# Weight operands made in two lanes, q's softmax with one exp, and another distance ahead of TensorE's matmuls in the planner

## The chip, the cores and the metric

The kernel runs on one core of a Trainium2 chip. The metric is the time of one execution on the device in microseconds. A core has five engines that each work off their own instructions in order: TensorE (PE, matmuls), VectorE (DVE), ScalarE (ACT), GpSimd (POOL) and SyncE (SP, which here issues nearly all DMAs). They wait for each other by semaphores.

## The reference

```python
def _attn_ref(q, k, v):                      # 8 batches, 8 heads, 576 rows, 64 columns
    q_s = q - np.max(q, axis=-1, keepdims=True)
    q_s = np.exp(q_s)
    q_s = q_s / (np.sum(q_s, axis=-1, keepdims=True) + 1e-09)
    k_s = k - np.max(k, axis=2, keepdims=True)
    k_s = np.exp(k_s)
    k_s = k_s / (np.sum(k_s, axis=2, keepdims=True) + 1e-09)
    kv = np.einsum('bhsd,bhse->bhde', k_s, v)
    return np.einsum('bhsd,bhde->bhse', q_s, kv)
def _moe_ref(x, w_in, w_out):                # 4608 tokens, 512 to 2048 to 512
    r = np.maximum(x @ w_in, 0.0)
    return (r * r) @ w_out
def _moe2_ref(x, w_gate, w_val, w_out):      # 512 to 1536 to 512
    g = x @ w_gate
    return (g * (1.0 / (1.0 + np.exp(-g))) * (x @ w_val)) @ w_out
```

Attention's output, heads side by side, is the x of the first MLP, and its output the x of the second.

## The kernel before

**Tiles.** The 4608 tokens are nine blocks of 512. A float32 matrix is split into a high part (a cast to fp32r, on ACT) and a low part (what the cast left, on DVE); a product is then three matmuls: high by high, high by low, low by high (`mm3`, all of them on line 107). The weights arrive as 8-byte numbers, and `bits` makes float32 words of them (one ACT and three DVE operations on 128x512).

**Stages.** (1) A first block, whose order is written out by hand (`FIRST_BLOCK`): block 0's attention, the conversion of the first MLP's weights, block 0 through the first MLP. (2) The direct stage: blocks 1 to 4 through the first MLP, with attention of the later blocks in between. (3) The pairs: blocks 5 to 8, two and two, by a scheme that replaces eight products of quarter matrices by seven (`PRODUCTS`). It needs sums and differences of quarters of the weights as operands. (4) The second MLP with the same seven products, in five groups of blocks (`gated` for gate and val, then `out_stage`).

**Weight operands.** `prepare` makes the operands of the seven products from 34 sets: 16 of the first MLP (their words are in memory already), 12 of gate and val, 6 of the second `w_out`. For a set it loads two halves, makes words (`bits`), forms sums (`quarter_sums`, line 325 on DVE), splits (`parts`, called by `staged`: ACT line 287, DVE line 289) into a staging tile `wst`, and stores that to memory (`hd`, `ad` for the first MLP, `gvd`, `od` for the second). The sets go one after the other. Operands for the matmuls are fetched in 512 KB pieces (tiles `wu`, five slots, line 829) on SP's queue.

**The planner.** Stages 2 and 3 get their order from `Plan`: each unit of work is a chain of steps (engine, assumed duration, what it needs, what it frees), with a rank. `Plan.run` takes the step that could start earliest, and among steps of that engine within 0.3 the lowest rank. The matmuls of the main line have rank 3, attention's 2 and something, the weight operands 5. `after` is the time that the plan leaves between an engine's end and its successor on another engine: 0.9 ahead of any PE step. What the plan puts out is then the fixed order on all five engines. In `gated` of the first group (g == 0) `next(work, None)` issues what is left of `prepare`, six steps behind each product, its stores on ACT's queue.

**Attention in the plan.** `kv_unit`: maxima of k on DVE, a transpose on PE (line 598), a reduction, a transpose back (604), a subtraction on DVE, an exp on ACT (612), 24 matmuls (557). `q_unit`: maxima on DVE (642), eight exps of 128x64 on ACT with the maximum as bias and the sum as second output (647), a reciprocal, a product on POOL (654), four transposes (678), the matmuls with kv.

Of the kernel before, what the change touches and what calls it, by code (L numbers as in the profile page):

```python
# [22 lines left out]
def tile_linear_attention_two_mlps(  # L23
# [30 lines left out]
    def f32(ap):  # L54
        return ap.bitcast(F32)
# [140 lines left out]
    class Plan:  # L196
# [26 lines left out]
        def start(self, u):  # L223
            engine, _, needs, take = u[2][:4]
            s = max(self.free[engine], u[3] + self.after(u[4], engine))
            for x in needs:
                if x not in self.done:
                    return None
                t, e = self.done[x]
                s = max(s, t + self.after(e, engine))  # L230
            for pool, key in take:
                bufs, keys = self.pools[pool]
                n = len(keys) - bufs
                if n >= 0:
                    x = pool, keys[n]
                    if x not in self.done:
                        return None
                    t, e = self.done[x]
                    s = max(s, t + self.after(e, engine))
# [40 lines left out]
    made = set()  # L280
    prep = {"stages": [(stp, "wst")] + [(raws, "raw0"), (raws, "raw1")], "raws": [], "n": 0, "r": 0}
# [9 lines left out]
    def staged(source, dests, by_rows=False, free=(), key=None):  # L291

        k_ = len(dests)
        pool, tag = prep["stages"][prep["n"] % len(prep["stages"])]
        prep["n"] += 1
        keep = (tag, prep["n"])
        prep["last"][tag] = [prep["n"]]
        t = []

        def make():  # L300
            t.append(pool.tile([P, 2, 2, U], F32R, name="wst", tag=tag))
# [19 lines left out]
    def quarter_sums(m, n, by_rows):  # L321
# [5 lines left out]
        yield step("DVE", 0.8)  # L327
# [6 lines left out]
        yield step("DVE", 0.8)  # L334
# [7 lines left out]
    def half_words(n):  # L342
        return cv.tile([P, T], F32, name="wsum", tag=f"wb{n}")

    def prepare():

        sets = [
            (kind + "1", f)
            for half in range(2) for kind in ("in", "out") for f in range(half * NM // 2, (half + 1) * NM // 2)
        ]  # L350
        sets += [x for f in range(NG) for x in (("gate", f), ("val", f))] + [("out", f) for f in range(NG)]
        loaded = {}

        def first_load(s, x):
            kind, f = sets[s]
            yield step("SP", 0.6, (), [(f"wb{x}", s)], (), [("ld", s, x)], 4.0)
            loaded[s, x] = half_words(x)
            nc.sync.dma_start(loaded[s, x], w1d[kind[:-1]][f][:, x])

        def raw(s, x):  # L360
            kind, f = sets[s]
            w, by_rows = {"gate": (w_gate, False), "val": (w_val, False), "out": (w_out2, True)}[kind]
            tag = prep["raws"][prep["r"] % len(prep["raws"])]
            prep["r"] += 1
# [4 lines left out]
            loaded[s, x] = t, keep  # L369

        def bits(s, x):
            yield step("ACT", 0.67, [("ld", s, x)], [(f"wb{x}", s)])
            t, keep = loaded.pop((s, x))
# [3 lines left out]
            w = cv.tile([P, T], I32, name="wbits", tag=f"wb{x}")  # L377
            nc.scalar.activation(f32(w), f32(high), AF.Copy, scale=2.0**-112)
            yield step("DVE", 0.5)
# [11 lines left out]
            loaded[s, x] = f32(w)  # L391

        for x in (0, 1):
            yield from first_load(0, x)
        for s, (kind, f) in enumerate(sets):
            first = kind[-1] == "1"
            more = s + 1 < len(sets)
            if not first and not prep["raws"]:
                prep["stages"].remove((raws, "raw0"))
                prep["raws"].append("raw0")  # L400
                plan.pools["raw0"] = [1, []]
                yield step("DVE", 0.05, [("st", *sets[s - 1], x) for x in range(2)])
                yield from aside(raw(s, 0))
            if len(prep["raws"]) == 1 and prep["plan"] and ("x1", NB - 1, NP - 1) in plan.done:
                prep["stages"] += [(qtp, "qT0"), (qtp, "qT1")]
                plan.pools.update(qT0=[1, []], qT1=[1, []])
                yield step("DVE", 0.02, [("raw1", n) for n in prep["last"]["raw1"]])
                prep["stages"].remove((raws, "raw1"))
                prep["raws"].append("raw1")
                plan.pools["raw1"] = [1, []]  # L410
            keys = [("wb0", s)], [("wb1", s)]
            if first:
                yield step("DVE", 0.02, [("ld", s, 0), ("ld", s, 1)])
                m, n = loaded.pop((s, 0)), loaded.pop((s, 1))
                by_rows = kind == "out1"
                yield from quarter_sums(m, n, by_rows)

                def to(name):
                    return first_to(kind[:-1], f, name)

                todo = ((m, ("6", "5")), (n, ("4", "7"))) if by_rows else ((m, ("7", "3")), (n, ("5", "6")))
                for x, (source, names) in enumerate(todo):
                    yield from staged(source, [to(name) for name in names], False, keys[x], ("st", kind, f, x))
                    if more and sets[s + 1][0][-1] == "1":
                        yield from aside(first_load(s + 1, x))
            else:
                by_rows = kind == "out"
                yield from bits(s, 0)
                yield from aside(raw(s, 1))
                m = loaded.pop((s, 0))  # L430
# [6 lines left out]
                def out_of(source, names, free=(), key=None):  # L437
                    return staged(source, [to(name) for name in names], by_rows, free, key)
# [5 lines left out]
                yield from bits(s, 1)  # L444
# [1218 lines left out]
```

## Time and profile before

| | |
|---|---|
| time, median of 3 runs | 1724.65 us (1724.08 to 1727.84) |
| the profiled execution | 1727.46 us, span 1725.7 us |
| PE, DVE, ACT, POOL busy | 1651.0, 1116.6, 961.1, 223.2 us |
| first block ends, pairs begin, second MLP begins | about 125, 585.4 and 909.1 us |
| granted TensorE clock, mean | 0.99 |

PE is busy for 96% of the span, and its matmul records are pipelined, so busy is not the same as at its peak. What is lost is to be looked for stretch by stretch: where PE waits, and where its clock is not 1.00.

### The profile page before, as it was taken

The numbers are of one execution on the slowest core, as the hardware profiler recorded it, in microseconds if no ns is written. First come the engines' busy times: TensorE is split into PE (matmuls) and PEld (weight loads), VectorE is DVE, ScalarE is ACT, GpSimd is POOL, SyncE is SP. The second block draws the span as 40 slices with busy tenths as digits, with TensorE's granted clock in tenths as the row PEclk, the third lists the DMA queues.
The fourth block names the chain that finished last, engine by engine and source line by source line (L and its number), as shares of the span: only waits on it lengthen the run. The fifth ranks groups of instructions, "written<-read, shape, count | busy, mean of one in ns | idle before, by whom it ended". The sixth has DMA issues, their size and how long they took to land.

```text
span 1725.7 us, 24332 instructions
## 1 busy us (share of the span) xinstructions
PE 1651.0 (96%) x8210; PEld 1348.8 (78%) x8210; DVE 1116.6 (65%) x1923; ACT 961.1 (56%) x1972; POOL 223.2 (13%) x206
## 2 busy tenths in 40 slices
PE   7998899999989999999998789999999999999998
PEld 5777677777867878778786578888888888888898
DVE  8875454655557566887688867744774476456656
ACT  7775566665656885767565445433543354334434
POOL 4760000000000100000001111011101110111020
PEclk9999999999999999999999899999999999999999
DMA  9956686774556779898988788876786668666897
GB/s 302 285 171 187 183 240 200 210 241 136 164 166 212 227 249 339 329 324 283 364 298 297 268 280 280 246 214 192 218 251 209 196 217 255 202 193 207 248 390 264
DMA packets 275020, 420.02 MB, mean 243 GB/s; under 512 B 126288, under 2 KB 167248, under 8 KB 274896
## 3 DMA queue, kind: packets, MB, share of 16 engines
q1 hardware_dynamic: 268736, 408.10, 74.2%
q10 hardware_dynamic: 6160, 10.36, 1.6%
q8 instruction: 66, 1.08, 0.2%
q14 instruction: 58, 0.48, 0.1%
HBM read 317.19 MB, written 101.19 MB: 242 GB/s over the span
## 4 chain that ended last, share of the span: by engine, by line
PE 75%; ACT 6%; DMA 5%; DVE 5%; issue 2%; POOL 1%; SPq 0%; ACTq 0%; DVEq 0%; POOLq 0%
PE ps L107 56%; PE ph L107 9%; PE acc L107 6%; PE pa L557 1%; ACT qs L647 1%; PE pa L107 1%; DMA wu<-gvd 1%; DMA gvd<-wst 1%; ACT r L724 1%; DMA od<-wst 1%; ACT r L722 1%; ACT g L287 1%; DMA vt<-in_v_dram 1%; PE pa L678 1%; ACT wst L287 0%
## 5 line engine op out<-in xcount | busy, mean ns | idle before, releaser
L107 PE MATMUL ps<-w,wu 128*128 128x512 f32 (+1 forms) x3192 | 687.9, 377 | 26.2 <-DMA wu<-gvd 15.5
L107 PEld LDWEIGHTS ps<-w,wu 128*128 128x128 f32 x3192 | 570.1, 191 | 140.4 <-ACT ps L1235 7.0
L107 PE MATMUL ps<-uo,wu 128*128 128x512 f32 (+1 forms) x1932 | 418.3, 378 | 0.3 <-DVE uo L1097 0.3
L107 PEld LDWEIGHTS ps<-uo,wu 128*128 128x128 f32 x1932 | 345.6, 188 | 71.4 <-DVE uo L1097 2.1
L107 PE MATMUL ph<-xT,w 128*128 128x512 f32 x960 | 250.6, 404 | 0.6 <-DVE xT L1487 0.3
L107 PE MATMUL acc<-g,w 128*128 128x512 f32 x960 | 245.4, 400 | 0.8 <-DVE g L1509 0.8
L107 PEld LDWEIGHTS ph<-xT,w 128*128 128x128 f32 x960 | 178.4, 191 | 41.5 <-DVE xT L1487 0.9
L107 PEld LDWEIGHTS acc<-g,w 128*128 128x128 f32 x960 | 177.9, 190 | 40.5 <-DVE g L1509 1.2
L101 ACT CAST uo<-u 128x512 fp32r<-128x512 f32 (+1 forms) x210 | 119.9, 579 | 111.6 <-PE ps L107 42.4
L1288 POOL TENSOR_TENSOR u<-u 128x512 f32<-128x512 f32 (+1 forms) x30 | 35.5, 1185 | 958.4 <-DVE u L1284 958.4
L1283 DVE TENSOR_TENSOR u<-u,ps 128x512 f32<-128x512 f32 (+1 forms) x60 | 37.9, 632 | 184.5 <-ACT u L1282 184.4
L102 DVE TENSOR_TENSOR uo<-u,uo 128x512 fp32r<-128x512 f32 (+1 forms) x210 | 133.0, 651 | 31.8 <-ACT uo L101 31.6
L1235 ACT COPY ps<-ps 128x512 f32<-128x512 f32 x126 | 72.1, 574 | 128.7 <-PE ps L107 124.1
L289 DVE TENSOR_TENSOR g<-r,g 128x512 fp32r<-128x512 f32 x64 | 44.3, 692 | 117.1 <-ACT g L287 117.1
L654 POOL TENSOR_TENSOR qs<-qs,qr 128x512 f32<-128x512 f32 x28 | 32.0, 1142 | 462.6 <-DMA gvd<-wst 80.4
L1097 DVE TENSOR_TENSOR uo<-u,uo 128x512 fp32r<-128x512 f32 x112 | 73.3, 686 | 23.6 <-ACT uo L1095 23.4
L722 ACT ACTIVATE r<-ph 128x512 f32<-128x512 f32 x64 | 38.3, 598 | 88.2 <-PE ph L107 87.7
L1095 ACT CAST uo<-u 128x512 fp32r<-128x512 f32 x112 | 66.4, 620 | 23.8 <-PE ps L107 22.7
L647 ACT ACTIVATE qs<-qs,qm 128x64 f32<-128x64 f32 x224 | 75.1, 337 | 7.7 <-DVE qm L642 5.2
L287 ACT CAST wst<-wbits 128x512 fp32r<-128x512 f32 (+1 forms) x72 | 51.0, 715 | 36.8 <-DVE wbits L388 22.4
L289 DVE TENSOR_TENSOR wst<-wbits,wst 128x512 fp32r<-128x512 f32 (+1 forms) x72 | 56.4, 789 | 22.2 <-ACT wst L287 20.6
L1282 ACT ACTIVATE u<-ps 128x512 f32<-128x512 f32 (+1 forms) x60 | 33.3, 555 | 49.7 <-PE ps L107 48.1
(186 smaller groups left out, 1780.7 us busy)
## 6 DMA issues: line engine op xcount, KB each, us to landing
wu<-gvd SPq DMA_DIRECT2D x210, 512.0 KB, 4.5
wu<-od SPq DMA_DIRECT2D x105, 512.0 KB, 4.1
wu<-hd SPq DMA_DIRECT2D x56, 512.0 KB, 6.0
wu<-ad SPq DMA_DIRECT2D x56, 512.0 KB, 4.8
gvd<-wst SPq DMA_DIRECT2D x84, 256.0 KB, 4.0
od<-wst ACTq DMA_DIRECT2D x39, 256.0 KB, 4.8
w<-in_moe_w_in_dram SPq DMA_DIRECT2D x16, 512.0 KB, 6.4
w<-in_moe_w_out_dram SPq DMA_DIRECT2D x16, 512.0 KB, 6.8
```

The lines of the kernel that those rows point to most:

```text
L101: nc.scalar.copy(hi, src)
L102: (eng or nc.vector).tensor_tensor(lo, src, f32(hi), op=ALU.subtract)
L107: nc.tensor.matmul(ps, lhsT=w[s], rhs=x[t], start=start and n == 0, stop=stop and n == 2, skip_group_check=more,)
L287: nc.scalar.copy(hi, src)
L289: nc.vector.tensor_tensor(lo, src, f32(hi), op=ALU.subtract)
L647: nc.scalar.activation(t[:, x, h], t[:, x, h], AF.Exp, bias=m[:, x, h:h + 1], accum_out=r[:, x, h:h + 1])
L722: nc.scalar.activation(r, ph, AF.Relu)
L1095: nc.scalar.copy(t[:, 0], src())
L1097: nc.vector.tensor_tensor(t[:, 1], src(), f32(t[:, 0]), op=ALU.subtract)
L1235: nc.scalar.copy(x, y)
L1283: nc.vector.tensor_tensor(u, u, gate, op=ALU.mult)
L1288: nc.gpsimd.tensor_tensor(s1, a21, a22, op=ALU.add)
```

## The change

1. The weight operands are made in two lanes that draw from the same list (`Lane`, `lane_one`, `lane_two`) instead of one after the other. The second lane has its words in `raw0` first; once the last q is through it uses q's tiles and a tile of kv (`qs`, `qT0`, `qT1`, `kvs`). Each lane alternates between two staging tiles.
2. All 34 sets stand in the plan (the added `plan.run` over all stores): none is left for `gated`.
3. In `q_unit` POOL adds the negated maxima, one exp of 128x512 runs on ACT, and DVE sums.
4. `after` gives 0.4 ahead of PE steps of rank 3, and 1.7 ahead of the others, instead of 0.9. Some assumed durations of DVE, PE and POOL steps change by 0.02 to 0.2.

```diff
-        def after(self, engine, other):
+        def after(self, engine, other, rank):
             if engine is None or engine == other:
                 return 0.0
-            return {"PE": 0.9, "SP": 1.0}.get(other, 0.2)
+            return {"PE": 0.4 if rank == 3 else 1.7, "SP": 1.0}.get(other, 0.2)
...
+    to_do = iter(sets)
+    class Lane:
+        def __init__(self, halves, raw, stages):
+            self.halves, self.raw, self.stages = halves, raw, stages
+            self.n = 0
+        def stage(self):
+            self.n += 1
+            return self.stages[self.n % len(self.stages)]
...
+    def lane_one():
+        yield from lane_a.first_sets()
+        yield step("DVE", 0.02, [("st", "out1", NM - 2, 1), ("st", "out1", NM - 1, 1)])
+        yield from lane_a.second_sets()
+    def lane_two():
+        yield from lane_b.first_sets()
+        yield step("DVE", 0.02, [("x1", NB - 1, NP - 1)])
+        lane_a.stages = [lane_a.stages[0], slot(qtp, "qT0")]
+        kv_slot = kvs[0].rearrange("p a b c -> p (a b c)").rearrange("p (k h n) -> p k h n", k=2, h=2)
...
+        lane = Lane(
+            [("qs", q_spare), ("qs", q_spare)], "raw1",
+            [slot(qtp, "qT1"), ("kvs", lambda: kv_slot)],
+        )
+        yield from lane.second_sets()
...
         m = sp.tile([P, TJ, 2], F32, name="qm", tag="qm")
         nc.vector.tensor_reduce(m, t, axis=AX.X, op=ALU.max, negate=True)
+        yield step("POOL", 1.2)
+        nc.gpsimd.tensor_tensor(t, t, m.unsqueeze(3).to_broadcast([P, TJ, 2, D]), op=ALU.add)
+        yield step("ACT", 0.63)
+        nc.scalar.activation(t, t, AF.Exp)
+        yield step("DVE", 0.68)
         r = sp.tile([P, TJ, 2], F32, name="qr", tag="qr")
-        for x in range(TJ):
-            yield step("ACT", 0.6)
-            for h in range(2):
-                nc.scalar.activation(
-                    t[:, x, h], t[:, x, h], AF.Exp, bias=m[:, x, h:h + 1], accum_out=r[:, x, h:h + 1]
-                )
+        nc.vector.tensor_reduce(r, t, axis=AX.X, op=ALU.add)
...
-        plan.unit(work, 5, 10.0)
+        for lane in lanes:
+            plan.unit(lane, 5, 8.0)
...
+            plan.run([("st", kind, f, x) for kind, f in sets for x in range(2)])
             plan.finish(4.9)
```

The order on PE in the direct stage, from one transpose of k's maxima (line 598) to the kv matmuls (557), before; `ph` and `acc` are the main line, in matmuls of 128x512:

```order
L598 MATMUL pa<-ident,m_1962 128x96
L107 MATMUL ph<-xT,w 128x512 x6
L107 MATMUL pa<-qT,kv_180 128x128 x3
L107 MATMUL pa<-qT,kv_179 128x384 x3
L604 MATMUL pa<-ident,mx 96x128
L107 MATMUL ph<-xT,w 128x512 x6
L107 MATMUL acc<-g,w 128x512 x12
L557 MATMUL pa<-vt,kt 64x65 x12
```

and now the same piece (lines 660, 666 and 619 in the new numbering):

```order
L660 MATMUL pa<-ident,m_1958 128x96
L107 MATMUL acc<-g,w 128x512 x9
L107 MATMUL pa<-qT,kv_180 128x128 x3
L107 MATMUL pa<-qT,kv_179 128x384 x3
L666 MATMUL pa<-ident,mx 96x128
L107 MATMUL acc<-g,w 128x512 x3
L107 MATMUL ph<-xT,w 128x512 x12
L107 MATMUL acc<-g,w 128x512 x6
L619 MATMUL pa<-vt,kt 64x65 x12
```

Between the two transposes there were 6 matmuls of the main line and are 9; between the second and the kv matmuls 18, now 21. Over the 24 units of the plan the means are 7.0 and 9.5 for the first distance (23 of them now), 14.4 and 18.9 for the second (one of 54 left out), and from q's transposes to the matmuls with kv 12.2 and 15.4.

SP's queue where the pairs end, before: `x2d` are the last stores of the pairs, `od` those of the weight operands, `wu<-gvd` the first fetches of the second MLP.

```order
L829 DMA wu<-gvd_166 128x1024 x2
L1150 DMA x2d_126<-st_8482 128x1024
L829 DMA wu<-gvd_166 128x1024
L115 DMA wraw<-in_moe_w_out_dram 128x512
L1150 DMA x2d_127<-st_8494 128x1024
L317 DMA od_172<-wst 128x512
L115 DMA wraw<-in_moe_w_out_dram 128x512
L317 DMA od_175<-wst 128x512
L317 DMA od_177<-wst 128x512
L829 DMA wu<-gvd_166 128x1024 x2
```

and now, from the fourth fetch on:

```order
L891 DMA wu<-gvd_166 128x1024
L1212 DMA x2d_127<-st_8507 128x1024
...
L326 DMA od_175<-wst 128x512
L326 DMA od_177<-wst 128x512
L326 DMA od_174<-kv_179 128x512
L326 DMA od_173<-kv_179 128x512
L326 DMA od_178<-wst 128x512
L326 DMA od_176<-wst 128x512
L891 DMA wu<-gvd_166 128x1024 x3
L891 DMA wu<-gvd_167 128x1024 x7
```

Before, three stores stand between the fourth and the fifth fetch, loads of further sets come behind, and 39 more stores are on ACT's queue. Now twelve stores stand there (the six shown and six before them), and no others behind.

DVE in the same place, its last rows ahead of the second MLP's own, now; `w<-x` and `x<-x` are that MLP's first operands, the rest are weight operands:

```order
L1024 TENSOR_TENSOR x<-x 128x512
L299 TENSOR_TENSOR wst<-wsum,wst 128x2x128x2
L405 SCALAR_TENSOR_TENSOR qs<-wraw,qs 128x512
L299 TENSOR_TENSOR w<-x,w 128x512
L409 SCALAR_TENSOR_TENSOR qs<-wraw,qs 128x512
L299 TENSOR_TENSOR w<-x,w 128x512
L299 TENSOR_TENSOR wst<-wsum,wst 128x2x128x2
L299 TENSOR_TENSOR wst<-qs,wst 128x2x128x2
L334 TENSOR_TENSOR qs<-qs 128x256 x4
L299 TENSOR_TENSOR kv_179<-qs,kv_179 128x2x128x2
L299 TENSOR_TENSOR wst<-qs,wst 128x2x128x2
```

From the last operation that the pairs' end releases (line 1237 now, 1175 before) to the second MLP's first (1345, before 1283) DVE has five splits of x, two differences of x, two word operations, six splits by rows (128x2x128x2) and eight sums. Before it had six splits of x, two differences, three word operations, two splits by rows (one of them half as large) and four sums.

## Rows read from the trace of the kernel before

**Rows 1.** windows by stage: stretch, length, busy us (instructions), PEclk, DMA share, GB/s

```profile
125.00:585.40 460.40, 432.75 (x2430) 343.47 (x2428) 265.52 (x560) 294.33 (x812) 27.69 (x24) 0.99 0.64 191
585.40:909.10 323.70, 319.09 (x1381) 256.56 (x1381) 239.25 (x351) 219.21 (x352) 4.27 (x4) 1.00 0.90 313
909.10:1058.90 149.80, 126.98 (x506) 100.44 (x505) 113.51 (x174) 73.34 (x113) 21.25 (x15) 0.92 0.78 272
```

**Rows 2.** timeline of PE, second MLP, second group; start, length, instructions

```profile
1115.98 114.40 PE L107 MATMUL ps<-w,wu 128*128 128x512 f32 x504
```

**Rows 3.** waits of PE, 909.1 to 1058.9; total us, times, longest

```profile
PE ps L107 <- DMA wu<-gvd: 15.5, 5, 5.8
```

**Rows 4.** timeline of all engines, 909 to 926

```profile
909.10 3.83 PE L107 MATMUL ps<-w,wu 128*128 128x512 f32 x16
...
909.30 1.22 DVE L1175 TENSOR_TENSOR st<-st,ps 128x1024 f32<-128x1024 f32 x1 [0.64 <-PE ps L107]
...
919.29 1.13 DVE L289 TENSOR_TENSOR wst<-wbits,wst 128x512 fp32r<-128x512 f32 x1 [0.95 <-ACT wst L287]
...
920.45 0.80 SPq L317 DMA_DIRECT2D od<-wst  x2
...
921.34 0.90 SPq L829 DMA_DIRECT2D wu<-gvd  x2
```

**Rows 5.** DMA issues, the page: queue, count, KB each, us to landing

```profile
od<-wst ACTq DMA_DIRECT2D x39, 256.0 KB, 4.8
```

**Rows 6.** timeline of PE, 915 to 1045, behind one wait for a fetch

```profile
925.72 19.06 PE L107 MATMUL ps<-w,wu 128*128 128x512 f32 x72 [4.04 <-DMA wu<-gvd]
```

**Rows 7.** windows of 2 us on PE; stretch, length, busy (instructions), granted clock

```profile
927.00:929.00 2.00, 2.00 (x6) 0.50 0.99 321
```

**Rows 8.** waits of PE, 125 to 600

```profile
PE pa L557 <- ACT kt L612: 10.2, 8, 1.8
PE pa L678 <- POOL qs L654: 8.4, 7, 1.9
PE pa L598 <- DVE m L595: 3.3, 6, 1.2
PE pa L604 <- DVE mx L601: 3.2, 5, 0.9
```

**Rows 9.** chain of waits: start, length, what; a slow stretch, an ordinary one

```profile
483.80 5.23 PE ph L107 x15
489.02 2.80 PE acc L107 x12
```

**Rows 10.** lines by form, ACT, 125 to 925: count, busy us, mean ns

```profile
L647 ACT ACTIVATE qs<-qs,qm 128x64 f32<-128x64 f32 x224 | 75.1, 337 | 7.7 <-DVE qm L642 5.2 <-issue 1.5 <-DMA vt<-in_v_dram 1.0
```

**Rows 11.** lines by form in the first block, 0 to 125: ACT's

```profile
L1448 ACT ACTIVATE qs<-qs 128x512 f32<-128x512 f32 x4 | 2.5, 619 | 0.0
```

**Rows 12.** lines by form in the first block, 0 to 125: DVE's

```profile
L1450 DVE TENSOR_REDUCE qr<-qs 128x8 f32<-128x512 f32 x4 | 2.7, 678 | 0.0
```

**Rows 13.** lines by form, DVE, 603 to 909

```profile
L325 DVE TENSOR_TENSOR wbits<-wbits 128x256 f32<-128x256 f32 x32 | 13.5, 423 | 0.7
L384 DVE SCALAR_TENSOR_TENSOR wbits<-wraw,wbits 128x512 int32<-128x512 int32 x16 | 11.0, 689 | 0.3
```

**Rows 14.** one line's instructions each: least, median, most ns

```profile
L654 POOL TENSOR_TENSOR qs<-qs,qr x28: 1042/1045/1674, 150.9 to 617.8; 128x512 f32<-128x512 f32 x28
...
L592 DVE TENSOR_TENSOR m<-kt x24: 501/546/1398, 132.2 to 527.8; 96x384 f32<-96x384 f32 x24
```

**Rows 15.** timeline of all engines, 289 to 293

```profile
290.04 1.05 POOL L654 TENSOR_TENSOR qs<-qs,qr 128x512 f32<-128x512 f32 x1 [15.43 <-PE acc L107]
290.11 1.39 DVE L592 TENSOR_TENSOR m<-kt 96x384 f32<-96x384 f32 x1
```

**Rows 16.** one wait of DVE, 603 to 909, and the window

```profile
DVE wst L289 <- ACT wst L287: 14.6, 11, 2.7
...
603.00:909.10 306.10, 302.24 (x1303) 242.73 (x1302) 229.90 (x332) 205.10 (x312) 2.09 (x2) 1.00 0.90 313
```

More of the change, by code (lines that the diff above doesn't have):

```diff
@@ L280, in tile_linear_attention_two_mlps, with aside @@
     made = set()
+    prep = {"n": 0, "issue": nc.sync, "plan": True}
+    def aside(steps):
+        if prep["plan"]:
+            plan.unit(steps, 4.9, plan.now)
+        else:
+            yield from steps
+    made = set()
     prep = {"stages": [(stp, "wst")] + [(raws, "raw0"), (raws, "raw1")], "raws": [], "n": 0, "r": 0}
@@ L333, in quarter_sums @@
             tt(c, c, d, ALU.add)
-        yield step("DVE", 0.8)
+        yield step("DVE", 0.92)
         if by_rows:
@@ L390, in bits @@
             )
[L391 to L412, printed above, removed]
+            self.loaded[s, x] = half
@@ new lines, in first_sets @@
+                    free = [(tag, s)] if self.halves[1][0] or x else ()
+                    to = [first_to(kind[:-1], f, name) for name in names]
+                    yield from staged(self.stage(), source, to, False, free, ("st", kind, f, x))
+                    if more and self.halves[1][0]:
+                        yield from aside(self.load(more, x))
+                if more and not self.halves[1][0]:
+                    yield from aside(self.load_two(more))
+                made.add(s)
@@ L457, in prepare, with slot, half_slot, first_half @@
                 for x, (source, names) in enumerate(todo):
-                    yield from out_of(source, names, keys[x], ("st", kind, f, x))
-            made.add((kind, f))
-    work = prepare()
+                    yield from out_of(source, names, [(self.halves[x][0], s)], ("st", kind, f, x))
+                made.add(s)
+                s = more
+    left, done = [], []
+    def slot(pool, tag):
+        return tag, lambda: pool.tile([P, 2, 2, U], F32R, name="wst", tag=tag)
+    def half_slot(tag):
+        return tag, lambda: cv.tile([P, T], F32, name="wsum", tag=tag)
+    both = []
+    def first_half():
+        both[:] = [f32(raws.tile([P, 2, T], F32R, name="wsum", tag="raw0"))]
+        return both[0][:, 0]
+    lane_a = Lane([half_slot("wb0"), half_slot("wb1")], "raw0", [slot(stp, "wst"), slot(raws, "raw1")])
+    lane_b = Lane([("raw0", first_half), (None, lambda: both[0][:, 1])], None, lane_a.stages)
+    def lane_one():
[7 more added lines that the diff above has]
+        kv_slot = kvs[0].rearrange("p a b c -> p (a b c)").rearrange("p (k h n) -> p k h n", k=2, h=2)
+        yield step("DVE", 0.02, [("raw1", keys[-1]) for keys in (plan.pools["raw1"][1],)])
+        lane = Lane(
[3 more added lines that the diff above has]
+        yield from lane.second_sets()
+    lanes = [lane_one(), lane_two()]
+    work = (x for steps in lanes for x in steps)
     def first_to(kind, f, name):
```

129 lines of the change are left out of this document (72 added, 57 removed).

## The prediction

> **What bounds the kernel now.** I read the windows by stage first. In the direct stage PE is busy for 432.75 of 460.40 us, in the pairs for 319.09 of 323.70, and in the first group of the second MLP's gate and val products (909.1 to 1058.9) for 126.98 of 149.80, at a mean clock of 0.92 [rows 1]. So the losses sit in two places. What the third stretch should take stands in the second group: the same 504 matmuls, with nothing to prepare beside them, take 114.40 us [rows 2], 0.227 each. The first group takes 149.8, so 35.4 us are lost there. The waits name fetches of operands first, 15.5 us in five waits [rows 3]. The timeline shows how one arises: the pairs end at 909.10, DVE's last operation for them starts at 909.30, a split of weight operands ends at 919.29 + 1.13 = 920.42, SP stores it at 920.45, and only then, at 921.34, issues the fifth fetch [rows 4]. PE has had four tiles until then, and goes on at 925.72 [rows 6]. The clock comes on top: after this wait it was granted at 0.50, the lower of the two levels, 1.2 GHz [rows 7], and the 72 matmuls behind it took 19.06 us [rows 6] where 72 x 0.227 = 16.3 would do, 2.7 us more.
>
> In the direct stage PE waits for attention: 10.2 us for the exp of k, 8.4 for POOL's product, 3.3 and 3.2 around the two transposes, 25.1 in all, in 26 waits [rows 8]. The clock is lost here as well: 15 matmuls took 5.23 us, where 12 take 2.80, so 15 take 3.5 [rows 9]; three stretches like this one make about 5 us.
>
> **The change part by part.** The sum is made against the profiled execution, 1727.46 us.
>
> *Attention's distance.* The plan now leaves 1.7 where it left 0.9, and the order shows it: 2.5, 4.5 and 3.2 more matmuls of the main line stand between attention's matmuls and what they wait for. At 2.80 / 12 = 0.233 us [rows 9] that is 0.6, 1.05 and 0.75 us. The mean wait is 25.1 / 26 = 0.97, the longest 1.9 [rows 8]. Taking 1.05 us from each of the 8 waits for the exp leaves 2.6 of 10.2 (the longest keep up to 0.75), taking 0.8 from the 7 for POOL leaves about 3, and 0.6 to 0.8 from the 11 others leaves 1.3: some 7 of 25.1. Main matmuls are put 0.5 closer to their producers (0.4 for 0.9); they waited for nothing worth a row, and this may cost up to 2 us.
>
> *q's softmax.* ACT loses eight exps of 337 ns a unit [rows 10] and gets one of 619 [rows 11], 2.1 us less, 58 us over 28 units. It was not the bound (294.33 of 460.40 us), so this is worth nothing by itself, but attention's chain queues behind less on ACT. DVE gets a sum of 678 ns a unit [rows 12], 28 x 0.68 = 19 us, and POOL a second operation of 1.05 us at the median [rows 14]. DVE also gets weight operands earlier, by the order 12 sums, 15 word operations, 7 whole and 3 half splits, about 20 us. It goes from 265.52 to some 305 of 460 us, 66%. What this adds to attention's latency I set at 1 us over the stage.
>
> What POOL's 28 operations do to DVE has bounds. Beside one of them, from 290.04 to 291.09, a maximum of k that started at 290.11 took 1.39 us [rows 15]; its median is 0.546 [rows 14]. So each can hold up DVE by 0 to 0.85 us: 0 to 24 us of DVE's time. Between these ends I take a third, 8 us, since the median of both operations is at their least; spread over the stage, with the longer distance, it reaches PE as 1 us. The Trainium skill has the rule ("SBUF — State Buffer", section "Who interferes with whom"): an operation of VectorE with two inputs in SBUF and one of GpSimd that reads SBUF lock each other out for a whole instruction. The trace agrees, 1.39 us against 0.546. By that rule alone every overlap would count in full, and it makes the second rival below.
>
> So the waits go from 25.1 to 10, and about 3 of the 5 us of lost clock go with them: **-18 us**, with bounds of -30 (every wait and all the clock) and +4 (DVE's load and the closer main matmuls, and no wait shorter).
>
> *Weight operands in the pairs.* Ahead of the last operation of the pairs DVE gets 16 more word operations and 4 more sums, five more whole splits and three more half ones, and 12 whole ones are by rows. A word operation is 0.689 us or less, a sum 0.423 [rows 13], a split by rows 1.13 [rows 4]: 16 x 0.6 + 4 x 0.42 + 8.7 + 2.4 = 22.5 us. From 603 to 909 DVE was busy for 229.90 of 306.10 us [rows 16], now 252, 82%. PE's waits there are small (319.09 of 323.70 busy). The plan assumes 0.62 and 0.70 for splits that take 1.13, so its order runs late on both engines where w_out is prepared. Bounds: -4 us (the waits there vanish) and +42 (the fourth case below). I take **+3**, near the low end, because 18% of DVE stays idle and the splits come at the lowest rank.
>
> *The hand-over.* All of the weight work behind 925 is gone, but not all of it is inside the pairs: DVE still has five splits of x and two differences, two word operations, six splits by rows and eight sums behind the last operation of the pairs, 9 x 0.69 + 6 x 1.13 + 8 x 0.42 = 16.4 us. Let the pairs end at 0. That last operation starts at 0.2 and takes 1.22 [rows 4]; DVE would be through at 17.8. The same sum for before gives 9.8 up to the split that SP waited for, which ended at 11.3: 1.5 us of waits for ACT. They stand here as well, 19.3. The last split also needs its tile back: the second lane's two tiles alternate, so its cast waits until the store of two splits earlier has landed, 4.8 us [rows 5]. That split ends at 13.9 in the sum, its store lands near 19, and cast and split by rows make it 21. SP's queue holds the twelve stores ahead of the fifth fetch. Before it took 0.9 us from the split's end to the fetch and 4.4 more to PE's start (921.34 to 925.72); so PE goes on at 21 + 0.9 + 4.4 = 26.3. The 48 matmuls of four tiles fill 10.9 of these: 15.4 lost, 2.7 for the clock, and 1 for the rest, 19 in place of 35.4: **-16.5 us**. Bounds: -32 if DVE is through in time for the four tiles to cover it (2 lost, no clock), -6 if it comes into the hand-over 10 us late. The middle value is the one worked out from rows.
>
> Sum: 1727.46 - 18 + 3 - 16.5 = 1696. The profiled execution lies 2.8 us above the median of 1724.65, so the median becomes **1693 us**.
>
> **The rivals.**
> 1. *The hand-over is worse, or DVE holds up PE in the pairs by some 12 us.* For it: DVE's order is fixed, and the assumed lengths of the splits are short by 0.4 to 0.5 us for 18 of them on each of two engines. Against it: the low rank of the weight work. 12 to 15 us above the forecast, 1707.
> 2. *Attention waits as before*, the main line's longer lead being used up by POOL's locks on DVE (24 us at the upper bound) and by DVE's 39 us more of work. For it: 26 waits of about 1 us, each about as long as one DVE operation. Against it: the added distance is as long as the mean wait. The direct stage gives nothing: 1693 + 18 = 1711.
> 3. *The change gets more:* the hand-over covered to within a few us, attention's waits nearly gone. 1693 - 12 - 8 = 1673. For it: the first set of stores is ready early. Against it: six splits by rows can't be done while PE works on four tiles.
> 4. *Slower: DVE's idle time in the pairs can't be used.* It was idle for 76.2 of 306.1 us [rows 16], and nearly all of that is waiting in order for ACT and PE, as 14.6 us for ACT's casts alone [rows 16]. If the idle time stays, 22.5 us of work lengthen the pairs by 22.5; eight more splits bring their own waits, 14.6 and 10 others over 32 splits, 0.8 each, 6 us; and PE stands in five pieces that cost 2.7 of clock each, 13: 42 in all, 39 more than I took. 1693 + 39 = 1732. It decides from about 32 us on. Against it: ACT loses work in the same stretch of time, and a wait in order is where a low rank puts its steps.
>
> **How the numbers follow.** The forecast 0.52 (1680 to 1703), rival 1 0.16, rival 2 0.13, rival 3 0.12, rival 4 0.07. From 1672 to 1713 about 0.85 lies inside: outside are rival 4 and the far half of rival 3. Less than 0.2% (3.4 us) can't be told from no change here. Slower by more: rival 4, 0.07. Within: 0.02, from the tails of rivals 2 and 4. Faster: 0.91.
>
> **What would show it.** In the profile of the changed kernel: the 504 matmuls behind the pairs take some 133 us, with one long wait for a fetch, 13 to 17 us after their start, behind SP's stores of `od`, one stretch at a clock of 0.50, and none of the later waits. A total without any such wait means that the hand-over was better covered than DVE's sum says. In the direct stage the waits for the exp of k and for POOL fall from 18.6 to 6 or 7 us; if they stay, rival 2 is right. In the pairs PE stays above 97% busy; waits for DVE's `uo` or `u` of more than a few us there speak for rivals 1 and 4. The forecast is wrong if the pairs lengthen by more than 10 us, or if the direct stage is not shorter by at least 8.

## The result and the profile after

| | before | after |
|---|---|---|
| time, median of 4 runs each on one chip | 1726.24 us (1724.08 to 1728.69) | 1679.20 us (1678.33 to 1681.57) |
| span of the profiled execution | 1725.7 us | 1676.6 us |
| direct stage | 460.4 us | 428.9 us |
| pairs | 323.7 us | 326.9 us |
| first group of 504 matmuls | 149.8 us | 129.1 us |
| first block and all behind the 504 | 791.8 us | 791.7 us |

The ratio is 0.9729, with a 95% interval of 0.9710 to 0.9748: 47 us faster. The forecast was 1693, with a range of 1672 to 1713. It was 14 us too high, and the measured time lies just below the 1680 to 1703 that it gave a chance of 0.52. The stages of the two profiled executions say where: the direct stage gave 31.5 us in place of 18, the pairs cost 3.2 in place of 3, the hand-over gave 20.7 in place of 16.5. (These add up to 49.0 us, as the two spans differ by 49.1; the medians differ by 47.)

These are the windows by stage of the kernel after, which answer to [rows 1]: stretch, length, busy us of PE, PE's weight loads, DVE, ACT and POOL with their instructions, granted clock, DMA share, GB/s.

```profile
125.00:553.93 428.93, 424.01 (x2432) 340.98 (x2430) 300.57 (x621) 251.56 (x459) 55.24 (x49) 1.00 0.73 221
553.93:880.80 326.87, 319.23 (x1377) 254.95 (x1376) 261.62 (x384) 225.86 (x313) 8.10 (x7) 1.00 0.93 331
880.80:1009.91 129.11, 117.18 (x505) 96.06 (x504) 71.25 (x108) 51.00 (x82) 19.28 (x15) 0.96 0.67 209
```

In the direct stage the length less PE's busy time went from 27.65 to 4.92 us, and busy time fell by 8.7 at the same work. In the pairs DVE's busy time rose by 22.4 us (239.25 to 261.62), PE's did not change, and the stage grew by 3. In the third stretch DVE has 71 us of work where it had 113.5.

The waits of PE in the direct stage, which answer to [rows 8] (total us, times, longest):

```profile
PE pa L619 <- ACT kt L674: 2.3, 2, 1.6
PE pa L666 <- DVE mx L663: 0.8, 1, 0.8
```

L619 is the line that was 557, L666 was 604. The 26 waits of 25.1 us are down to three of 3.1; the one for POOL is gone altogether. So is the lost clock: before, windows of 24, 12 and 24 us from 281, 413 and 473 were granted 0.93, 0.86 and 0.93 in the mean, which is 24 x 0.07 + 12 x 0.14 + 24 x 0.07 = 5.0 us; after, both halves of the stage are at 1.00.

The hand-over, from the timeline of the kernel after, 880 to 906 (start, length, engine, line; in brackets the idle time before and what ended it). It answers to [rows 4, 6].

```profile
880.80 3.96 PE L107 MATMUL ps<-w,wu 128*128 128x512 f32 x16
881.00 1.22 DVE L1237 TENSOR_TENSOR st<-st,ps 128x1024 f32<-128x1024 f32 x1 [1.03 <-PE ps L107]
...
884.64 9.82 SPq L326 DMA_DIRECT2D od<-wst  x8
886.16 7.54 PE L107 MATMUL ps<-w,wu 128*128 128x512 f32 x32 [1.40 <-DVE w L299]
896.82 1.07 ACT L297 CAST wst<-qs 128x512 fp32r<-128x512 f32 x1 [0.70 <-DMA od<-wst]
897.26 0.80 SPq L326 DMA_DIRECT2D od<-kv  x2
...
897.93 1.08 DVE L299 TENSOR_TENSOR wst<-qs,wst 128x512 fp32r<-128x512 f32 x1 [0.69 <-ACT wst L297]
899.04 0.79 SPq L326 DMA_DIRECT2D od<-wst  x2
899.93 2.48 SPq L891 DMA_DIRECT2D wu<-gvd  x5
904.24 2.04 PE L107 MATMUL ps<-w,wu 128*128 128x512 f32 x4 [10.54 <-DMA wu<-gvd]
```

This is the chain that the prediction drew. The last cast waits for its tile, until a store has landed; the split follows and ends at 899.01; SP issues the twelfth store, and then the fifth fetch; PE goes on 4.3 us after that. The split ends 18.2 us after the pairs, where 21 was forecast, and PE resumes at 23.4 in place of 26.3. One wait for a fetch is left, of 10.5 us, and the clock behind it is at the lower level, 1.2 GHz, for 4 us, as in [rows 7] (windows of 2 us):

```profile
904.00:906.00 2.00, 1.76 (x4) 1.49 (x5) 0.00 (x0) 0.00 (x0) 0.00 (x0) 0.50 1.01 408
906.00:908.00 2.00, 2.00 (x6) 1.53 (x5) 0.69 (x1) 0.10 (x1) 0.00 (x0) 0.50 1.03 422
908.00:910.00 2.00, 2.00 (x8) 1.57 (x8) 1.22 (x2) 0.53 (x1) 0.00 (x0) 0.75 0.17 70
```

The 504 matmuls now take 129.1 = 114.4 without a loss [rows 2] + 11.9 of waits + 2.8 of busy time beyond it (117.18 for 114.4), most of it the clock.

### The profile page after: what moved, and what is told of

Read it like the earlier page. It is cut to its first block, busy times and chain, and to the rows that moved or that the text cites. A ratio compares the mean times of both kernels' runs of the same rounds, so it can differ in the third digit from the quotient of the medians.

```text
span 1676.6 us, 23953 instructions
## 1 busy us (share of the span) xinstructions
PE 1632.3 (97%) x8210; PEld 1340.4 (80%) x8210; DVE 1132.4 (68%) x1951; ACT 902.8 (54%) x1552; POOL 252.5 (15%) x234
## 4 chain that ended last, share of the span: by engine, by line
PE 83%; DMA 4%; DVE 4%; ACT 2%; issue 1%; SPq 1%; POOL 0%; DVEq 0%; ACTq 0%; POOLq 0%
PE ps L107 59%; PE ph L107 11%; PE acc L107 10%; PE pa L619 1%; DMA wu<-hd 1%; DMA od<-wst 1%; PE pa L107 1%; DVE wst L299 1%; PE pa L740 1%; DMA gvd<-wst 0%; DVE wsum L334 0%; DMA w<-in_moe_w_out_dram 0%; ACT wst L297 0%; DVE uo L1159 0%; ACT u L1113 0%
## 5 line engine op out<-in xcount | busy, mean ns | idle before, releaser
L107 PE MATMUL ps<-w,wu 128*128 128x512 f32 (+1 forms) x3192 | 678.7, 374 | 16.8 <-DMA wu<-gvd 10.5
L107 PE MATMUL ph<-xT,w 128*128 128x512 f32 x960 | 246.7, 400 | 1.1 <-ACT xT L297 0.6
L297 ACT CAST wst<-wsum 128x512 fp32r<-128x512 f32 (+1 forms) x88 | 58.5, 666 | 37.5 <-DVE wsum L409 18.4
L706 POOL TENSOR_TENSOR qs<-qs,qm 128x512 f32<-128x512 f32 x28 | 30.9, 1103 | 305.2 <-DVE qm L704 185.8
L299 DVE TENSOR_TENSOR wst<-wsum,wst 128x512 fp32r<-128x512 f32 (+1 forms) x88 | 66.1, 753 | 7.9 <-ACT wst L297 6.6
L1306 ACT COPY p<-ps 128x512 f32<-128x512 f32 x63 | 36.9, 587 | 44.8 <-PE ps L107 44.2
```

What stands on the lines that cost most here:

```text
L107: nc.tensor.matmul(ps, lhsT=w[s], rhs=x[t], start=start and n == 0, stop=stop and n == 2, skip_group_check=more,)
L297: nc.scalar.copy(hi, src)
L299: nc.vector.tensor_tensor(lo, src, f32(hi), op=ALU.subtract)
L1306: nc.scalar.copy(x, y)
```

## The experiments

Eleven kernels were run beside the kernel before. The lengths are those of the profiled execution in us; PE waits are the sum in the direct stage and in the 504.

| | total | against before | direct | pairs | 504 | PE waits |
|---|---|---|---|---|---|---|
| before | 1726.2 | 1 | 460.4 | 323.7 | 149.8 | 27.3, 22.9 |
| after | 1679.2 | 0.9729 | 428.9 | 326.9 | 129.1 | 4.4, 11.9 |
| e1_distance_back | 1695.6 | 0.9820 | 447.7 | 328.3 | 125.5 | 18.4, 6.7 |
| e2_old_q | 1696.6 | 0.9826 | 433.7 | 328.4 | 144.0 | 5.8, 26.2 |
| e3_lanes_alone | 1714.2 | 0.9922 | 451.3 | 327.5 | 143.6 | 19.0, 27.0 |
| e4_main_line_back | 1677.8 | 0.9714 | 435.4 | 322.6 | 127.3 | 7.2, 9.7 |
| e5_stores_on_pool | 1671.5 | 0.9679 | 431.9 | 327.7 | 121.3 | 4.7, 3.6 |
| e6_fifth_fetch | 1677.6 | 0.9719 | 429.9 | 329.2 | 127.2 | 4.5, 10.0 |
| e7_durations_alone | 1719.3 | 0.9960 | 450.6 | 327.1 | 148.6 | 21.8, 22.9 |
| e8_q_on_dve | 1674.5 | 0.9701 | 432.5 | 333.3 | 114.6 | 8.0, 0 |
| e9_q_alone | 1712.9 | 0.9922 | 459.3 | 325.7 | 137.3 | 28.6, 13.4 |
| e10 | 1668.9 | 0.9670 | 435.7 | 323.5 | 117.0 | 7.2, 2.4 |
| e11 | 1667.4 | 0.9659 | 433.9 | 328.2 | 114.6 | 8.9, 0 |

The intervals of the ratios reach 0.0014 to 0.0024 to either side, 2.5 to 4 us. How well a stage's length repeats is seen from after, e5 and e6, in which PE's order is the same: the direct stage took 428.9, 431.9 and 429.9 us, the pairs 326.9, 327.7 and 329.2. So a difference of up to 3 us in one stage of one execution says nothing.

**e1: the planner's distance ahead of PE back at 0.9, all else as after.**

```diff
-            return {"PE": 0.4 if rank == 3 else 1.7, "SP": 1.0}.get(other, 0.2)
+            return {"PE": 0.9, "SP": 1.0}.get(other, 0.2)
```

> The changed kernel with one edit undone: the plan leaves 0.9 ahead of every PE step again; lanes, q's softmax and the assumed durations stay. The order has 6.0, 15.9 and 12.4 main matmuls in attention's three distances (after: 9.5, 18.9, 15.4). Theory D (the direct stage's gain is the distance): PE's waits for attention there come back to 15 to 25 us from 4.4, with some lost clock, and the stage is 15 to 22 us longer than the 428.9 of the changed kernel. Theory Q (the gain is ACT's freed queue, by q's single exp): the waits stay under 8 us, the stage within 5 us. By either, 10 stores instead of 12 stand ahead of the fifth fetch behind the pairs, so the hand-over takes about what it took. D: about 1697 us, Q: about 1683.

PE's waits in its direct stage:

```profile
PE pa L660 <- DVE m L657: 6.6, 5, 2.1
PE pa L619 <- ACT kt L674: 4.3, 5, 1.3
PE pa L740 <- POOL qs L716: 3.1, 4, 1.5
```

14 of the waits' 23 us come back, and the direct stage is 18.8 us longer: the distance is the largest single part there. The 504 are a little shorter without it (125.5: the one wait for a fetch is 4.7 us in place of 10.5).

**e2: q's old softmax (eight exps on ACT), all else as after.**

```diff
-        yield step("POOL", 1.2)
-        nc.gpsimd.tensor_tensor(t, t, m.unsqueeze(3).to_broadcast([P, TJ, 2, D]), op=ALU.add)
-        yield step("ACT", 0.63)
-        nc.scalar.activation(t, t, AF.Exp)
...
+        for x in range(TJ):
+            yield step("ACT", 0.6)
+            for h in range(2):
+                nc.scalar.activation(
...
```

> The changed kernel with q's softmax undone: eight exps of 128x64 with the maximum as bias; lanes and distance stay. The distances in the order are 9.1, 18.2 and 16.2 main matmuls, as in the changed kernel. Theory D: the direct stage's waits stay under 8 us and its length within 4 us of 428.9. Theory Q: the waits come back to 15 us or more. By either the hand-over behind the pairs is worse: the order has over 17 stores and a load ahead of the fifth fetch (12 in the changed kernel), so at 0.8 us for a pair of stores and 1.1 for a split by rows I expect the wait for that fetch to be 15 to 30 us instead of 10.5. D: 1685 to 1700 in all.

The queue of SP in this kernel, from its timeline behind the pairs (they end at 887.12):

```profile
889.71 0.32 SPq L326 DMA_DIRECT2D od<-wst  x1
894.61 0.79 SPq L326 DMA_DIRECT2D od<-kv  x2
899.19 6.16 SPq L326 DMA_DIRECT2D od<-wst  x6
905.44 0.40 SPq L115 DMA_DIRECT2D wraw<-in_moe_w_out_dram  x1
906.38 0.32 SPq L326 DMA_DIRECT2D od<-kv  x1
907.75 7.57 SPq L326 DMA_DIRECT2D od<-wst  x4
918.26 0.80 SPq L326 DMA_DIRECT2D od<-kv  x2
919.61 0.82 SPq L326 DMA_DIRECT2D od<-wst  x2
920.53 2.62 SPq L891 DMA_DIRECT2D wu<-gvd  x5
```

18 stores and a load stand ahead of the fifth fetch, which goes out 33.4 us after the pairs where after it takes 19.1; PE waits 25.2 us for it. The one exp is worth 4.8 us in the direct stage and 15 at the hand-over: the weight operands come later in the order, with ACT's load in the direct stage at 297.6 us in place of 251.6. That ACT's load is the reason is argued and not isolated: e8 below shortens the 504 by as much, 14.5 us, with ACT's load as it was (253.3 us for 251.6).

**e3: both of these back, so that the lanes and the new assumed durations stand alone.** Its edit is that of e1 and that of e2.

> The changed kernel with distance and q's softmax both undone: the two lanes, all sets in the plan, and the assumed durations are left of the change. Distances 7.4, 14.2 and 11.0, as in the kernel before (7.0, 14.4, 12.2). D: the direct stage is at the length of before, 455 to 465 us; Q: the same, since neither is there. If it is below 450 the assumed durations or the lanes themselves shorten the waits, a third theory (T). Over 16 stores ahead of the fifth fetch: the gate and val stretch stays near 140 us. D and Q: 1710 to 1720 in all, T: 1695 to 1705.

At 451.3 us the direct stage is 9 us shorter than before, though the distances ahead of attention's matmuls are those of before. That is below the 455 to 465 of theories D and Q, and just above the 450 below which theory T was to hold. The 504 take 143.6, with one wait of 25.6 us: the lanes by themselves bring little at the hand-over.

**e4: the main line's steps (rank 3) at 0.9, attention's at 1.7.**

```diff
-            return {"PE": 0.4 if rank == 3 else 1.7, "SP": 1.0}.get(other, 0.2)
+            return {"PE": 0.9 if rank == 3 else 1.7, "SP": 1.0}.get(other, 0.2)
```

> The changed kernel with 0.9 instead of 0.4 ahead of the main line's PE steps (rank 3); 1.7 for the others stays. Distances 8.6, 18.5 and 15.5. D: the direct stage stays within 3 us of 428.9. If the 0.4 had cost waits of the main line they would go, but there were only 0.8 us of them. Theory H (the hand-over is as long as the weight operands that the plan leaves behind the pairs): only 7 stores stand ahead of the fifth fetch instead of 12, so its wait falls from 10.5 us to 3 to 7, and the total from 1679 to about 1674. Without H nothing changes.

The 0.4 gains 6.5 us in the direct stage and costs 4.3 in the pairs and 1.8 in the 504: nothing that can be told in the total (1677.8 for 1679.2, intervals that overlap). Seven stores stand ahead of the fifth fetch in place of twelve, and still PE waits 9.3 us for it, where theory H had 3 to 7. The last split and the fetch in its timeline (the pairs end at 883.05):

```profile
898.07 1.08 DVE L299 TENSOR_TENSOR wst<-qs,wst 128x512 fp32r<-128x512 f32 x1 [0.31 <-ACT wst L297]
900.09 2.68 SPq L891 DMA_DIRECT2D wu<-gvd  x5
```

The split ends 16.1 us after the pairs in place of 18.2, and PE goes on at 904.50, 21.5 after them in place of 23.4: it is the end of the last split that counts, not the number of stores.

**e5: the stores of the last two sets of `w_out` from POOL's queue.**

```diff
-            yield step("SP", 0.6 * k_, done, (), [keep], [key] if key else (), 4.0)
+            engine, queue = ("POOL", nc.gpsimd) if late else ("SP", prep["issue"])
+            yield step(engine, 0.6 * k_, done, (), [keep], [key] if key else (), 4.0)
             for j, to in enumerate(dests):
-                prep["issue"].dma_start(to, f32(t[0][:, j]))
+                queue.dma_start(to, f32(t[0][:, j]))
```

> The changed kernel, but the `od` stores of the last two sets of w_out operands go out from POOL's DMA queue, so that SP's queue holds no store between the fourth and the fifth fetch of the second MLP. Theory Q (the 10.5 us wait at the hand-over is SP's queue: the fifth fetch stands in order behind twelve stores, the last of which wait for DVE's split): the fetch is issued before the pairs end, the wait of 10.5 us falls below 2.5, the stretch at a clock of 0.50 behind it goes, the 504 matmuls take 114 to 118 us in place of 129.1, the total 1665 to 1669. Theory W (DVE is late with the weight operands themselves, and the wait only moves to the set that is made last): the fetch comes early, but a wait of 5 to 10 us stands one or two tiles later, the 504 matmuls take 124 to 130 us, the total 1675 to 1680.

SP's queue and PE in its timeline (the pairs end at 884.60), and the waits that are left in the 504:

```profile
884.60 3.96 PE L107 MATMUL ps<-w,wu 128*128 128x512 f32 x16
...
886.05 0.32 SPq L1213 DMA_DIRECT2D x2d<-st  x1
886.46 1.41 SPq L892 DMA_DIRECT2D wu<-gvd  x2
```

```profile
PE ps L107 <- DVE u L1346: 1.9, 1, 1.9
PE ps L107 <- DVE w L299: 1.4, 1, 1.4
PE ps L107 <- DVE s L1315: 0.3, 1, 0.3
```

The fifth fetch goes out 1.9 us after the pairs, 17 us earlier, and the wait for it is gone: it was the queue. The gain is 7.8 us in the 504, less than the 11 to 15 of theory Q. Theory W's wait of 5 to 10 us for a later fetch did not come. What is left are 3.6 us of waits for DVE's operations of the second MLP itself, of which 1.4 stood in after too. The last, of 1.9 us up to 911.65, is for an operation that stands behind the last split; that split ends 25.3 us after the pairs here, in place of 18.2, since two casts wait 3.6 and 3.9 us until a store from POOL's queue has landed. The lower clock comes back behind this wait (windows of 2 us):

```profile
912.00:914.00 2.00, 2.00 (x9) 1.60 (x8) 2.00 (x5) 2.00 (x5) 0.00 (x0) 0.80 0.85 307
914.00:916.00 2.00, 2.00 (x6) 1.59 (x5) 2.00 (x4) 0.28 (x2) 0.74 (x1) 0.50 0.37 148
916.00:918.00 2.00, 2.00 (x9) 1.57 (x8) 1.08 (x1) 0.80 (x2) 1.92 (x2) 0.85 0.51 106
```

PE is busy for 117.5 us in the 504, 3 more than without a loss, of which these windows are (0.20 + 0.50 + 0.15) x 2 = 1.7.

**e6: one more fetch in the plan, ahead of the twelve stores.**

```diff
-            for n in range(self.n_pairs + 4):
+            for n in range(self.n_pairs + 5):
```

> The changed kernel with one more fetch in the plan, so that the fifth fetch of the second MLP stands ahead of the twelve stores and the sixth behind them. Both theories: PE has five tiles in place of four when it comes to the stores, one tile is 12 matmuls or 2.7 us, so the wait of 10.5 us becomes about 8, the 504 matmuls take 126 to 127 us in place of 129.1, the total 1676 to 1678. If the wait disappears altogether, the stores were never what the fifth fetch waited for, and theory Q falls.

As expected: the wait is 8.6 us, the 504 take 127.2. The last split ends 18.6 us after the pairs, as it did (18.2), and a tile ahead of the stores is worth 1.9 us, no more than its 12 matmuls (2.7).

**e7: the kernel before with only the new assumed durations.**

```diff
-        yield step("DVE", 0.62)
+        yield step("DVE", 0.82)
         nc.vector.tensor_tensor(m1, m3[:, :, 0], m3[:, :, 1], op=ALU.max)
...
-        yield step("PE", 0.15, (), [("pa", me)])
+        yield step("PE", 0.17, (), [("pa", me)])
```

> The kernel before with nothing but the new assumed durations of DVE's and PE's steps (0.92 for 0.8 and the like). Theory T (the 9 us that the direct stage gained without the new distance and without the new q come from steps put where the engines really reach them): the direct stage takes 449 to 454 us in place of 460.4, PE's waits there 17 to 21 us in place of 27.3. Theory L (they come from the weight operands in two lanes, which take weight work out of the places where attention's steps stand): the direct stage stays at 457 to 463. In both the 504 matmuls stay at 145 to 153 us, and the total follows the direct stage: 1712 to 1720 under T, 1722 to 1730 under L.

The windows of its direct stage and its pairs:

```profile
125.00:575.60 450.60, 428.43 (x2430) 341.95 (x2429) 266.78 (x560) 294.64 (x811) 28.49 (x24) 1.00 0.65 195
575.60:902.69 327.09, 319.46 (x1381) 256.64 (x1380) 238.54 (x350) 219.45 (x354) 4.95 (x4) 1.00 0.90 310
```

The numbers by which the planner places steps, and nothing that is computed, make the direct stage 9.8 us shorter: 5.5 of them are waits (27.3 to 21.8), 4.3 busy time, of which 3.3 is clock (one stretch of 24 us at 0.93 is left of three). That is as much as the 9 us of e3, so the lanes gave the direct stage nothing that can be told (in e3 the waits fell further, to 19.0, and all three stretches of lower clock are there). The pairs lose 3.4 of it.

**e8: q's maxima taken off by DVE in place of POOL.**

```diff
-        yield step("POOL", 1.2)
-        nc.gpsimd.tensor_tensor(t, t, m.unsqueeze(3).to_broadcast([P, TJ, 2, D]), op=ALU.add)
+        yield step("DVE", 0.7)
+        nc.vector.tensor_tensor(t, t, m.unsqueeze(3).to_broadcast([P, TJ, 2, D]), op=ALU.add)
```

> The changed kernel with q's maxima taken off by DVE in place of POOL (28 operations of about 1.1 us leave POOL, 28 of about 0.7 us, 20 us in all, come to DVE). Theory P (POOL's operations hold DVE up by the 8 us that the prediction took, 1 us of it on PE): no more than 3 us either way, 1677 to 1683, the medians of DVE's own operations in the direct stage unchanged. Theory K (POOL beside DVE costs DVE much more, up to 24 us): DVE's maxima of k become shorter in the mean by 0.1 us or more and the direct stage is 3 to 6 us shorter, 1673 to 1676. Theory B (DVE is near its bound in the direct stage and the pairs): 5 us or more slower, 1684 to 1692.

Four groups of DVE's lines in the direct stage, after:

```profile
L299 DVE TENSOR_TENSOR g<-r,g 128x512 fp32r<-128x512 f32 x64 | 46.5, 726 | 87.1 <-ACT g L297 87.0
L334 DVE TENSOR_TENSOR wsum<-wsum 128x256 f32<-128x256 f32 x88 | 39.7, 452 | 2.1 <-DMA wsum<-w1d_in 0.4
L299 DVE TENSOR_TENSOR wst<-wsum,wst 128x512 fp32r<-128x512 f32 x50 | 37.6, 755 | 3.4 <-ACT wst L297 2.4 <-DMA qs<-in_q_dram 0.7
L654 DVE TENSOR_TENSOR m<-kt 96x384 f32<-96x384 f32 x24 | 14.8, 615 | 1.8 <-DMA kt<-in_k_dram 1.8
```

and in e8:

```profile
L334 DVE TENSOR_TENSOR wsum<-wsum 128x256 f32<-128x256 f32 x92 | 46.0, 501 | 2.0 <-DMA wsum<-w1d_in 0.2
L299 DVE TENSOR_TENSOR g<-r,g 128x512 fp32r<-128x512 f32 x64 | 45.4, 709 | 82.0 <-ACT g L297 81.0 <-PE pa L740 0.5
L299 DVE TENSOR_TENSOR wst<-wsum,wst 128x512 fp32r<-128x512 f32 x53 | 37.1, 699 | 2.7 <-ACT wst L297 2.4 <-DMA ad<-w 0.2
L654 DVE TENSOR_TENSOR m<-kt 96x384 f32<-96x384 f32 x24 | 13.9, 581 | 0.3 <-DMA kt<-in_k_dram 0.2
```

Three of them get shorter, by 64 x 0.017 + 50 x 0.056 + 24 x 0.034 = 4.7 us, and the sums (line 334) get longer, by 88 x 0.049 = 4.3: the edit moved DVE's delays about and hardly took any away. The traces have the total. DVE's operations that overlap one of POOL's took 12.4 us more in the direct stage before, 15.7 after and 14.6 in e8 than by the median of operations of the same line, tiles and shape; those that overlap none took nothing more. So POOL does hold DVE up, 12.4 us by 24 operations before, but its second operation per unit added only 1 to 3 us of that, where the forecast took 8, and the direct stage doesn't get shorter without it (432.5 for 428.9). The Trainium skill ("SBUF — State Buffer", section "Who interferes with whom") calls the lock exclusive. By that rule alone the 28 added operations could have cost DVE up to their whole 30.9 us; the traces agree that operations which meet hold each other up, and show that in this order little of that came on top.

The total is 4.7 us lower than after all the same. That is the total of theory K, but its signs did not come: the maxima of k are 0.034 us shorter in the mean, not 0.1, and the stage is no shorter. The reason is one that none of the three theories had: the order is another. All stores of `od` stand ahead of the last post of the pairs, so the 504 run in one piece in 114.6 us, and the pairs are 6.4 us longer (one wait for a cast on ACT takes 4.8).

**e9: the kernel before with only q's new softmax.** Its edit is that of e2 the other way round.

> The kernel before with nothing but q's new softmax (maxima taken off by POOL, one exp). Theory A (ACT's relief is what moves weight work ahead of the hand-over, with or without lanes and distance): the direct stage is 4 to 8 us shorter (454 +- 3), and of the 11 loads of w_out that stood behind the pairs some three or four stand ahead of it, so the 504 matmuls take 138 to 144 us in place of 149.8; the total 1706 to 1715. Theory B (q's exp is worth something only with the lanes and the distance beside it): the direct stage 459 to 463, the 504 matmuls 147 to 152, the total 1722 to 1729.

At the hand-over it is theory A: 137.3 us, 12.5 less than before, without lanes or distance. In the direct stage nothing is gained (459.3). The waits there show why:

```profile
PE pa L598 <- DVE m L595: 12.4, 12, 2.2
PE pa L557 <- ACT kt L612: 8.6, 7, 2.3
PE pa L604 <- DVE mx L601: 2.8, 4, 1.0
PE pa L678 <- POOL qs L654: 2.6, 6, 0.9
```

Against [rows 8] the wait for POOL's product has fallen by 5.8 us, and the one for DVE's maxima of k has risen by 9.1: DVE has 297 us of work in place of 265.5.

**e10: the edits of e4 and e5 together.**

> The changed kernel with two edits together: the late `od` stores on POOL's queue, and the main line's own distance back at 0.9. From the single edits: the stores took 8 us off the 504 matmuls and left 3.6 us of waits for DVE, the main line gave the pairs 4 us and the direct stage cost 6. If they add up, the direct stage takes 433 to 436 us, the pairs 322 to 324, the 504 matmuls 118 to 122, the total 1667 to 1672. If DVE's weight operands are what is left, the 504 matmuls fall to 115 to 118 here, since 7 stores stand behind the pairs in place of 12 and DVE is through earlier.

They add up: 435.7, 323.5, and 117.0 us for the 504 at a clock of 1.00, with one wait of 2.4. With fewer stores left DVE is through earlier: its last split ends 19.7 us after the pairs, where it was 25.3 in e5.

**e11: the edit of e8, and the main line's distance at 0.6.**

> A version that should beat both: the changed kernel with q's maxima taken off by DVE, and the main line's distance at 0.6 in place of 0.4. In the order all stores of `od` now stand ahead of the last post of the pairs, two of them just ahead of it. If what counts is whether DVE's weight work is through when the pairs end, the 504 matmuls take 114.5 to 117 us without a wait for a fetch, the pairs 326 to 333 (PE's waits there below 11 us), the direct stage 430 to 434, the total 1667 to 1674. If the work that is pulled ahead of the hand-over is paid for in the pairs one for one, the pairs take 335 to 340 and the total 1675 to 1682.

The pairs' end and the 504 in the timeline of PE:

```profile
886.19 1.10 PE L107 MATMUL ps<-uo,wu 128*128 128x512 f32 x4
887.12 114.79 PE L107 MATMUL ps<-w,wu 128*128 128x512 f32 x504
```

1667.35 us (1666.98 to 1670.15), a ratio of 0.9659 (0.9645 to 0.9674): it beats both kernels, after by some 12 us; the two intervals don't meet. The hand-over costs nothing any more, since the last two stores of `od` go out at 887.16, ahead of the pairs' last post at 888.57; and the pairs take only 1.3 us more than after, with DVE busy for 80.8% of them (265.04 of 328.22).

## Why the prediction came out as it did

One edit at a time from before to after, by the runs that differ in it alone:

| edit | runs | direct | pairs | 504 | total |
|---|---|---|---|---|---|
| assumed durations | before, e7 | -9.8 | +3.4 | -1.2 | -6.9 |
| lanes | e7, e3 | +0.7 | +0.4 | -5.0 | -6.6 |
| distance | e3, e2 | -17.6 | +0.9 | +0.4 | -16.6 |
| q's softmax | e2, after | -4.8 | -1.5 | -14.9 | -16.7 |

Totals are differences of the ratios, times 1726.2; stages are of one execution each, so that a row adds up to within a few us. In another order a part can be worth more or less: q alone gives 13.5, the distance last 15.7. The row of the lanes also holds the plan over all stores (point 2 of the change) and one assumed duration of POOL's, which no run took apart; the row of the distance holds both of its edits, of which e4 shows the main line's.

- *Direct stage, -18: the step that was mis-sized.* It reads "the waits go from 25.1 to 10, and about 3 of the 5 us of lost clock go with them". Measured are -31.5, just outside its bound of -30: all waits of the stage -22.9 (27.3 to 4.4), clock -5.0, and 3.6 more of busy time that was not looked for. The mechanism was right, and the distance by itself gave 17.6, near the sum's 18, though in other parts: 15 of waits and 3 of clock there, 12.2 of idle time and 5.4 of busy time by the windows of e3 and e2. What was missing is the assumed durations. The prediction weighs only the splits' assumed lengths, as a risk in the pairs, and the change leaves those as they were; to the ones that do change it gave nothing, and here they are worth 9.8. The other miss was the +1 us each for DVE's load and POOL's locks, and up to 2 for the main line put closer; q's softmax shortened the stage by 4.8 once the distance was there, and the closer main line gained 6.5 (e4).
- *Pairs, +3.* Measured +3.2, and that is luck. DVE's added work, 22.5 us by the sum, is 22.4 in the windows, but the length does not follow it: e7 has none of it (238.5 us of DVE's time, 239.3 before) and its pairs are 3.4 longer, e4 has nearly all of it (260.1) and its are 1.1 shorter, and runs with one order on PE differ by 2.3. The added work went into DVE's idle time. The fourth rival, that it could not, is out: DVE reaches 80% of the stage, and 80.8% in e11.
- *Hand-over, -16.5.* Measured -20.7. Chain, queue and wait are those of the text; the last split ended 2.8 us earlier than the sum had it (18.2 for 21), which is most of the 4.2 us. The price of the clock, 2.7, came out at 2.8 as busy time. e5 shows that the fetch stood behind SP's stores; e4 and e6, that neither fewer stores nor one fetch more changes much while the last split ends when it does.
- *First rival* (a hand-over 12 to 15 us worse, or DVE holding PE up in the pairs): neither came. The hand-over is 4 us better than forecast, and PE's waits for DVE in the pairs are 2.9 us in all.
- *What the sum named as its cause was wrong in part.* The text has q's exp "worth nothing by itself", since ACT was not the bound. The order that the hand-over's sum was read from already held its effect, so the sum was right; but e9 and e2 put 12.5 to 15 us of the 20.7 on that exp, and 5 on the lanes. So an edit to an engine that bounds nothing set how early the weight operands stand in the order. That it did so by ACT's relief stays open, since e8 and e4 move the order at the hand-over by edits that leave ACT's work alone.
- *Second rival* (attention waits as before): it did not come (4.4 us of waits). With only q's part the waits stay, at 28.6 us for 27.3 (e9), so the distance and the durations are what took them away; POOL's locks cost 1 to 3 us more than before, not the 24 of the upper bound.
- *Third rival* (more gain): attention's waits nearly gone was right, the hand-over covered was not; its 1673 is 6 us below the measurement.

## What to carry to other kernels

Where a planner sets the order, its assumed durations are part of the change: they moved the direct stage by 9.8 us and the total by 6.9 here without any other edit, and should be given a term of their own. Price each edit against every stage that its order reaches, also one in which its engine is not the bound. And a load behind stores in one queue leaves when the last producer of these stores is done: move the stores (e5) or finish the producer (e8, e11), since one more load ahead (e6) or fewer stores (e4) gained 2 us or less.

## What the runs showed of the hardware beside that

The clock's price hung little on the length of the wait ahead of it. PE was busy for 116.6 to 118.7 us of the 504 in after, e1, e2, e3, e4 and e6, whose longest waits are 10.5, 4.7, 25.2, 25.6, 9.3 and 8.6 us, against 114.5 to 114.6 in e8, e10 and e11. The most, 118.7, is that of e1 with the shortest of these waits: its clock fell twice. And how long a wait must be for the clock to fall is not to be read from its length alone: behind 1.9 us in e5 it fell to 0.50, behind 2.4 us in e10 it stayed at 1.00 (windows of e10; the wait ends at 904.55):

```profile
902.00:904.00 2.00, 0.12 (x1) 0.00 (x0) 1.10 (x2) 1.98 (x2) 0.00 (x0) 1.00 0.95 307
904.00:906.00 2.00, 1.45 (x6) 1.23 (x7) 2.00 (x4) 1.99 (x5) 1.07 (x2) 1.00 0.72 283
906.00:908.00 2.00, 2.00 (x10) 1.62 (x10) 2.00 (x4) 0.68 (x2) 0.00 (x0) 1.00 0.71 191
```

In e5 two shorter waits (1.4 and 0.3 us) stand ahead of it in the same stretch, in e10 none. That this is the cause was not tried.
